# Two f blocks in one PSUM bank pair, transposes in other banks, and output products moved forward

## The chip, the cores and the metric

The kernel runs on one NeuronCore of a Trainium2 chip. The metric is the device time of one execution in microseconds (us), taken as the median of several runs. The engines have their own queues of instructions and meet only at semaphores: TensorE (PE) does the matmuls and its weight loads (PEld), VectorE (DVE), ScalarE (ACT) and GpSimd (POOL) the rest, and SyncE (SP) issues all large transfers, among them transposing ones. PE writes to PSUM, which has eight banks of 512 float32 columns here called 0 to 7; DVE and ACT read it.

## The reference

It is one transformer layer on 2048 tokens of width 448, with 16 heads of 28, in bf16. The first half is a linear attention whose features are two softmaxes, and the second a gated MLP of 1792 hidden columns:

```python
pq, pk = einsum(q, w_phi), einsum(k, w_phi)          # per head, 28 x 28
phi_q = concat([softmax(pq), softmax(-pq)]); phi_k = ...   # same for k
kv = einsum("bhsf,bhsd->bhfd", phi_k, v); z = einsum("bhsf->bhf", phi_k)
o = einsum("bhqf,bhfd->bhqd", phi_q, kv) / (einsum("bhqf,bhf->bhq", phi_q, z) + 1e-6)
h = x + o @ wo                                       # all of it on layernorm(x)
n = layernorm(h)
h2 = h + (sigmoid(n @ w_gate) * (n @ w_up)) @ w_down
```

## The kernel before, in words

The tokens are 16 tiles of 128, in four chunks of four tiles. Everything up to the sum kv (all keys and values) comes first, up to about 44 us. From there a tile passes through these named steps, whose names are those of the order lists:

- `pqa`/`pqb` c_i (function `pq`): the query features of chunk c, two groups of heads each, 512 columns, into banks 0 and 1 or 4 and 5. ACT takes two exponentials (`eq` with p or m) of the two banks together.
- `num` t: the products of a tile's query features with kv, into banks 6 and 7 (`num1` into 2 and 3). DVE makes `rsm`, `qq`, `b`, `c`, `rden` of it, and `o` t (DVE or POOL) writes the attention's output to o_pad. `oT` t transposes that, tiles 0 and 1 on PE, the others by a transfer that SP issues.
- `woa`/`wob` t: the output products of tiles t and t+1, banks 2 and 3. `h` t adds x (for tiles 0 and 1 the matmuls add it already); then come the second norm (`bs2`, `ag2` for tiles 0 and 1, `nm`, `sq`, `ve` for the others, `pow2` for the inverse root), `hn` t, and the transpose `hT` t, tiles 0 and 1 on PE, the others through SP.
- `ga`/`gb` t_f (function `gate_up`): gate and up products of one f block (128 of the 1792 hidden columns), 14 of them, for the tiles t on: tiles 0 and 1, and 2 and 3, in two phases of 256 tokens, the others in chunks of 512. Gate goes to bank 4 or 0, up to bank 5 or 1, by turns. `sig` t_f is a tanh on ACT into sg_sb (0.5 + 0.5 tanh(g/2) is the sigmoid), `hh` t_f on DVE makes (tanh + 1) times up, as bf16, in hhT.
- `dn`, `dp`, `dm` t_f (functions `down`, `down1`): the products with w_down, banks 2 and 3 for the early tiles, and `fin` t and `out` t, the second residual and the store.

Most products come as two halves. Matmuls use 64 rows of the array each, and two on opposite row halves run side by side (`both`, `pair`). The first half (`ga`, `pqa`, `woa`) has four such slots, with bank A on the low rows and bank B on the high rows; the second half (`gb`, ...) has three, with the rows swapped. A second half waits until the first half's matmuls into the same bank are complete (`crosses`, line 74).

The order on every engine is written out by hand in `ORDER` (lines 223 to 290). `PROGRAM` (line 292) gives the order in which steps are declared, and from that the waits come: a step waits for the last writer and the readers of each bank and tile that it writes, and the engines then go strictly by `ORDER`. So an instruction that waits holds back all that stand behind it on its engine.

In the phase of the first 256 tokens the order on PE is, with the gate products begun after both transposes:

```python
"pqa3_0 pqb3_0 wgu pqa3_1 num5 pqb3_1 hT1 hT0 num6 ga0_1 ga0_0 gb0_1 gb0_0 woa2 num7 ga0_2 ..."
```

The transposes `hT0`, `hT1` use banks 2 and 3, those of the output product just read. `wgu` does no work: it only makes PE wait for the gate and up weights.

Of the kernel before, what the change touches and what calls it, by code (L numbers as in the profile page):

```python
# [6 lines left out]
ALU = mybir.AluOpType  # L7
# [11 lines left out]
class Graph:  # L19
# [90 lines left out]
    def emit(self, nc):  # L110
# [85 lines left out]
P = 128  # L196
# [5 lines left out]
KT = 4  # L202
# [39 lines left out]
    ),  # L242
# [39 lines left out]
    ),  # L282
    "pool": (
# [5 lines left out]
    ),  # L289
}  # L290
PACE = {"ld_wg1": "kva14"}
PROGRAM = (
# [21 lines left out]

def pair(oa, ob, wa, wb, ra, rb):


    def f1(e):
        return both(e, [(oa, wa(LO, k), ra(LO, k), k == 0, False) for k in range(4)],
                    [(ob, wb(HI, k), rb(HI, k), k == 0, False) for k in range(4)])  # L320

    def f2(e):
        return both(e, [(ob, wb(LO, k), rb(LO, k), False, k == B_LO[-1]) for k in B_LO],
                    [(oa, wa(HI, k), ra(HI, k), False, k == A_HI[-1]) for k in A_HI])
    return f1, f2


def build(nc, A_x, A_wqkv, A_w_phi, A_wo, B_w_gate, B_w_up, B_w_down, out):
# [10 lines left out]
    with ExitStack() as es:  # L339
# [488 lines left out]
        def resid(t, b, ha=False):  # L828
# [27 lines left out]
            op("dve" if ha else ("dve", "pool"), "hn%d" % t, hnf, r=[("x", t), ("mv2", t) if ha else ("nm2", t), ("rst2", t)], w=[("hn", s)])  # L856
            if t < 2:
                pe_transpose("hT%d" % t, [hn_pad[:, s, kt * P:(kt + 1) * P] for kt in range(KT)], b, hnT[c][:, :, TS(t)],
                             ("hn", s), ("xnT", t))
            else:  # L860
                op("sp", "hT%d" % t, lambda e: e.dma_start_transpose(out=hnT[c][:, :, TS(t)], in_=hn_pad[:, s, :]),
                   r=[("hn", s)], w=[("xnT", t)], dma="tr", nring=64)

        def wout(t):
# [32 lines left out]
        for n, keys in (("wwo", wo_keys), ("wgu", wgu_keys)):  # L897
            op("pe", n, lambda e: None, r=keys, rows=64)
        sgn = [0]

        def gate_up(t0, n, ff):
            hb = hnT[t0 // 4]
            N = n * P
            ns = slice((t0 % 4) * P, (t0 % 4) * P + N)
            hk = [("xnT", t) for t in range(t0, t0 + n)]
            bg, bu = ((4, 5), (0, 1))[ff % 2]
            fs = slice(ff * P, (ff + 1) * P)
            nm = "%d_%d" % (t0, ff)
            f1, f2 = pair(bk(bg)[:, 0:N], bk(bu)[:, 0:N], lambda h, k: wg_sb[h, k, fs], lambda h, k: wu_sb[h, k, fs],
                          lambda h, k: hb[h, k, ns], lambda h, k: hb[h, k, ns])  # L910
            op("pe", "ga" + nm, f1, r=hk + wgu_keys, w=[B(bg), B(bu)], rows=64, half={bg: 0, bu: 1})
            op("pe", "gb" + nm, f2, r=hk + wgu_keys, w=[B(bg), B(bu)], rows=64, half={bg: 1, bu: 0})
            k = sgn[0] % NSG
            sgn[0] += 1
            op("act", "sig" + nm, lambda e: e.activation(sg_sb[:, k, 0:N], bk(bg)[:, 0:N], ACT.Tanh, scale=0.5), r=[B(bg)], w=[("sg", k)])  # L915
            op("dve", "hh" + nm, lambda e: e.scalar_tensor_tensor(out=hhT[(t0 // 4) % NHH][:, ff, ns], in0=sg_sb[:, k, 0:N], scalar=1.0,  # L916
                                                                  in1=bk(bu)[:, 0:N], op0=ALU.add, op1=ALU.mult),
               r=[B(bu), ("sg", k)], w=[("hh", (t0 // 4) % NHH, ff, t % 4) for t in range(t0, t0 + n)])

# [38 lines left out]
        for step in PROGRAM.split():  # L958
            k, _, v = step.partition(":")
            v = [int(i) for i in v.split(",") if i]  # L960
            if k == "num":
                num(*v)
            elif k == "wo":
                wout(v[0])
            elif k == "ot":
                otrans(v[0])
            elif k == "wo1":
                wout1(v[0])
            elif k == "qs":
                qsum(v[0])  # L970
            elif k == "pq":
                pq(*v)
            elif k == "kvz":
                kvmask()
            elif k == "gu":
                for ff in range(*(v[2:4] or (0, FT))):
                    gate_up(v[0], v[1], ff)
            elif k == "down":
                down(v[0], (v[1], v[1] + 1), mid)
            elif k == "down1":  # L980
                down1(v[0], v[1], late, *v[2:])
# [40 lines left out]
```

## Time and profile before

| | |
|---|---|
| median of 3 runs | 203.62 us (203.53 to 203.92) |
| profiled execution | 203.67 us, span 201.8 us |
| PE busy | 195.7 us, 97% of the span |
| DVE busy | 133.0 us, 66% |
| ACT busy | 91.3 us, 45% |
| POOL busy | 56.7 us, 28% |
| granted TensorE clock | 1.000 |
| gate products' start (`ga0_1`) | 59.24 us |
| first 512-column gate product (`ga4_1`) | 95.00 us |

The span is from the first to the last instruction. Times in the profile's rows count from the span's start. A row of the view in order of time has the start, the duration, the engine, the line, the operation, out<-in, and the count, and in brackets the idle time before it and what ended it. L311 is the helper through which all paired matmuls go, so the operands tell them apart: `xnT,Wq` are query products, `kvz,eq` nums, `wo_e` and `wo_o` output products, `xnT,wg_sb` and `xnT,wu_sb` gate and up, `wd_sb,hhT` down.

### The profile page before, as it was taken

How to read it: one execution, taken by the hardware profiler on the slowest of the kernel's cores; microseconds unless marked ns; L12 is line 12 of the kernel's file. 1: busy time of each engine (PE TensorE's matmuls, PEld its weight loads, DVE VectorE, ACT ScalarE, POOL GpSimd, SP SyncE). 2: the span in 40 equal slices, each digit the busy share in tenths (PEclk: the TensorE clock that was granted, in tenths of full speed). 3: DMA queues.
4: the chain of work that ended last, by engine and by line, in shares of the span. 5: the costliest groups of instructions: out<-in, count | busy, mean ns of one | idle time of the engine just before them, and what ended most of it. 6: DMA issues, size and time to landing. Idle time of an engine off the chain costs nothing.

```text
span 201.8 us, 5882 instructions
## 1 busy us (share of the span) xinstructions
PE 195.7 (97%) x2516; PEld 112.9 (56%) x2516; DVE 133.0 (66%) x320; ACT 91.3 (45%) x188; POOL 56.7 (28%) x97
## 2 busy tenths in 40 slices
PE   7999999999989999999999999999999999999995
PEld 3835656665558778676444444555555555554443
DVE  5999999978899677767758977436432422272224
ACT  2668898899772636222333442324422212222220
POOL 5879939433433614600041110001400000000000
PEclk9999999999999999999999999999999999999999
DMA  5965445839973320241005411030312000004003
GB/s 159 313 142 124 55 100 63 260 134 276 299 208 62 67 38 3 53 81 29 0 3 124 81 26 26 6 72 28 70 34 52 0 3 0 0 3 136 0 0 94
DMA packets 32491, 16.27 MB, mean 81 GB/s; under 512 B 24720, under 2 KB 31568, under 8 KB 32464
## 3 DMA queue, kind: packets, MB, share of 16 engines
q1 hardware_dynamic: 32336, 15.86, 32.4%
q8 instruction: 20, 0.33, 0.7%
q14 instruction: 7, 0.06, 0.1%
q10 hardware_dynamic: 128, 0.03, 0.1%
HBM read 8.34 MB, written 1.84 MB: 50 GB/s over the span
## 4 chain that ended last, share of the span: by engine, by line
PE 90%; ACT 2%; DVE 2%; DMA 2%; issue 1%; SPq 1%; POOL 1%
PE psum L311 83%; PE psum L943 5%; DMA wk_sb<-in_A_wqkv_dram 2%; ACT hhT L673 1%; ACT hhT L674 1%; PE psum L526 1%; PE psum L614 1%; SPq L415 1%; DVE st L831 1%; POOL rst L835 1%; PE psum L540 0%; DVE hn_pad L853 0%; DVE b_sb L803 0%; PE psum L601 0%; DVE c_sb L806 0%
## 5 line engine op out<-in xcount | busy, mean ns | idle before, releaser
L311 PE MATMUL psum<-xnT,wg_sb 64*128 64x512 bf16 (+1 forms) x490 | 93.1, 333 | 0.2
L311 PE MATMUL psum<-xnT,wu_sb 64*128 64x512 bf16 (+1 forms) x490 | 92.9, 333 | 0.0
L915 ACT ACTIVATE sg_sb<-psum 128x512 bf16<-128x512 f32 (+1 forms) x70 | 34.8, 511 | 91.3 <-PE psum L311 90.7
L916 DVE SCALAR_TENSOR_TENSOR hhT<-sg_sb,psum 128x512 bf16<-128x512 bf16 (+1 forms) x70 | 38.9, 576 | 54.5 <-ACT sg_sb L915 54.2
L311 PEld LDWEIGHTS psum<-xnT,wg_sb 64*128 64x128 bf16 x490 | 44.4, 94 | 22.5 <-DVE hhT L916 4.3
L311 PEld LDWEIGHTS psum<-xnT,wu_sb 64*128 64x128 bf16 x490 | 44.4, 94 | 13.0
L311 PE MATMUL psum<-wd_sb,hhT 64*128 64x448 bf16 x336 | 36.9, 349 | 0.0
L311 PEld LDWEIGHTS psum<-wd_sb,hhT 64*128 64x128 bf16 x336 | 17.6, 94 | 14.4 <-DVE x_sb L838 0.5
L311 PE MATMUL psum<-Wk,xnT 64*128 64x448 bf16 x112 | 22.2, 350 | 0.5 <-ACT hhT L674 0.2
L311 PE MATMUL psum<-wv_sb,xnT 64*128 64x448 bf16 x112 | 22.3, 351 | 0.1
L847 POOL TENSOR_SCALAR ve<-ssq 128x1 f32<-128x1 f32 x11 | 2.2, 201 | 55.0 <-ACT junk L844 54.8
L677 DVE TENSOR_REDUCE ss<-hhT 128x32 f32<-128x896 bf16 x16 | 16.9, 1066 | 0.6 <-ACT hhT L674 0.2
L723 ACT ACTIVATE eq<-psum 120x1024 bf16<-120x1024 f32 x16 | 15.7, 1024 | 1.0 <-PE psum L311 0.8
L687 POOL TENSOR_TENSOR phi<-hhT,rs 128x896 bf16<-128x896 bf16 x8 | 13.6, 1710 | 5.5 <-PE psum L311 5.1
L311 PE MATMUL psum<-xnT,Wq 64*120 64x512 bf16 x112 | 15.0, 384 | 0.1
L812 POOL TENSOR_TENSOR o_pad<-c_sb,rden 128x448 bf16<-128x448 bf16 x10 | 9.3, 935 | 14.9 <-DVE rden L808 14.8
L311 PE MATMUL psum<-wo_o,oT 64*128 64x448 bf16 x56 | 13.2, 349 | 0.0
L311 PE MATMUL psum<-wo_e,oT 64*128 64x448 bf16 x56 | 13.1, 349 | 0.0
L950 DVE SCALAR_TENSOR_TENSOR x_sb<-psum,x_sb 128x448 bf16<-128x448 f32 (+2 forms) x17 | 9.4, 592 | 2.7 <-PE psum L943 1.6
L943 PE MATMUL psum<-wd_sb,hhT 128*128 128x448 bf16 (+2 forms) x70 | 11.1, 316 | 0.0
L311 PEld LDWEIGHTS psum<-Wk,xnT 64*128 64x128 bf16 x112 | 7.8, 94 | 5.8 <-PE psum L311 1.0
L673 ACT ACTIVATE hhT<-psum 128x448 bf16<-128x448 f32 x16 | 8.8, 553 | 4.4 <-PE psum L311 4.2
(105 smaller groups left out, 235.4 us busy)
## 6 DMA issues: line engine op xcount, KB each, us to landing
out_dram<-x_sb SPq DMA_DIRECT2D x15, 112.0 KB, 1.8
x_sb<-in_A_x_dram SPq DMA_DIRECT2D x7, 224.0 KB, 3.9
wd_sb<-in_B_w_down_dram SPq DMA_DIRECT2D x7, 224.0 KB, 4.2
wg_sb<-in_B_w_gate_dram SPq DMA_DIRECT2D x3, 448.0 KB, 6.3
wu_sb<-in_B_w_up_dram SPq DMA_DIRECT2D x3, 448.0 KB, 6.7
wv_sb<-in_A_wqkv_dram SPq DMA_DIRECT2D x2, 224.0 KB, 4.7
wk_sb<-in_A_wqkv_dram SPq DMA_DIRECT2D x2, 196.0 KB, 3.8
wo_e<-in_A_wo_dram SPq DMA_DIRECT2D x1, 336.0 KB, 3.2
```

The lines of the kernel that those rows point to most:

```text
L311: p = e.matmul(o, lhsT=w, rhs=r, start=st, stop=sp, tile_position=(row, 0))
L415: return op(eng, name, lambda e: e.dma_start(dst, src), r=r, w=w, dma="in" if eng == "sp" else "ain", nring=48 if eng == "sp" else 8, kb=kb)
L673: e.activation(ek[:, s, :, 0, :], src, ACT.Exp)
L677: op("dve", "ss%d" % t, lambda e: e.tensor_reduce(ss[:, s, :].rearrange("p (b h) -> p b h", h=2), eks.rearrange("p b (d h) -> p b h d", h= ...
L687: return e.tensor_tensor(phi[:, sp, :, :, :].rearrange("p b a n -> p (b a) n")[:, :, 0:56].rearrange("p b (d h) -> p b d h", h=2), eks.rea ...
L723: op("act", "eq%d_%d%s" % (c, i, "pm"[sg]), lambda e, sg=sg: e.activation(eq[c][:, sg, 2 * i:2 * i + 2, :].rearrange("p g n -> p (g n)"), ...
L812: return e.tensor_tensor(o_pad[:, t % NO, off:off + D].rearrange("p (h d) -> p h d", h=H), c_sb[:, t % NS, :, 0:DH], rden[:, t % NS, :][:, ...
L847: op(("pool", "dve"), "ve%d" % t, lambda e: e.tensor_scalar(ve2[:, t:t + 1], ssq2[:, t:t + 1], 1.0 / D ** 3, EPS, op0=ALU.mult, op1=ALU.ad ...
L915: op("act", "sig" + nm, lambda e: e.activation(sg_sb[:, k, 0:N], bk(bg)[:, 0:N], ACT.Tanh, scale=0.5), r=[B(bg)], w=[("sg", k)])
L916: op("dve", "hh" + nm, lambda e: e.scalar_tensor_tensor(out=hhT[(t0 // 4) % NHH][:, ff, ns], in0=sg_sb[:, k, 0:N], scalar=1.0, in1=bk(bu)[ ...
L943: p = e.matmul(bk(b)[:, lo:hi], lhsT=hb[:, ff, TS(t)], rhs=wd_sb[:, ff, lo:hi], start=ff == 0, stop=ff == FT - 1)
L950: op("dve", "fin%d%s" % (t, nm), lambda e: e.scalar_tensor_tensor(out=h_sb[:, t, lo:hi], in0=bk(b)[:, lo:hi], scalar=0.5, in1=h_sb[:, t, l ...
```

## The change

In the two 256-token phases, an even and the next odd f block now share one bank pair: the even one uses columns 0 to 255 of the gate and the up bank, the odd one 256 to 511. The first matmul of the even block starts the banks, and the odd one's do not. The second halves `gb` of both blocks are declared after both first halves. One tanh and one `hh` of 512 columns then serve both, so `sig` and `hh` of odd f blocks are gone in these phases. The bank pairs go by turns of two blocks (4 and 5, then 0 and 1). The 512-token phases keep their form.

`hT0` and `hT1` move into a step of their own (`htrans`), declared after the query products of chunk 3's first groups, and use banks 0 and 1.

The order lists change from about 45 us to about 100 us: on PE `num1` stands before `pqb1_1`, `num4` between the halves of `pq3_0`, `num5` after `pqb3_1`, `woa2` before the first gate product, `num6` behind three of them, and `wgu` far back; the output products `woa`, `wob` and the down products come earlier among the gate products. DVE does the statistics, `hn` and transposes' copies of tile 1 before tile 0; ACT does `oT0e` one exponential earlier and `h1` before `h0`. `o7`, `hn2`, `hn3`, `nm2`, `nm3` and `ve3` go from POOL to DVE, and `o9`, `o10`, `ve5`, `ve7`, `nm5`, `nm9` and `hn7` from DVE to POOL. SP's order is the same.

```diff
-def pair(oa, ob, wa, wb, ra, rb):
+def pair(oa, ob, wa, wb, ra, rb, first=True, last=True):
...
-        return both(e, [(oa, wa(LO, k), ra(LO, k), k == 0, False) for k in range(4)],
+        return both(e, [(oa, wa(LO, k), ra(LO, k), first and k == 0, False) for k in range(4)],
...
-            if t < 2:
-                pe_transpose("hT%d" % t, [hn_pad[:, s, kt * P:(kt + 1) * P] for kt in range(KT)], b, hnT[c][:, :, TS(t)],
-                             ("hn", s), ("xnT", t))
-            else:
+            if t >= 2:
...
+        def htrans(t):
+            s = t % NH
+            pe_transpose("hT%d" % t, [hn_pad[:, s, kt * P:(kt + 1) * P] for kt in range(KT)], t, hnT[0][:, :, TS(t)], ("hn", s), ("xnT", t))
...
+            two = n == 2
-            bg, bu = ((4, 5), (0, 1))[ff % 2]
+            bg, bu = ((4, 5), (0, 1))[(ff // 2 if two else ff) % 2]
...
+            cs = slice(N * (ff % 2), N * (ff % 2) + N) if two else slice(0, N)
...
-            op("pe", "gb" + nm, f2, r=hk + wgu_keys, w=[B(bg), B(bu)], rows=64, half={bg: 1, bu: 0})
+            if two and ff % 2 == 0:
+                gate_up_b.append((nm, f2))
+                return
+            todo = gate_up_b + [(nm, f2)]
+            gate_up_b.clear()
+            for nb, fb in todo:
+                op("pe", "gb" + nb, fb, r=hk + wgu_keys, w=[B(bg), B(bu)], rows=64, half={bg: 1, bu: 0})
...
+            nm, W = todo[0][0], N * len(todo)
+            dst = hhT[(t0 // 4) % NHH][:, ff + 1 - len(todo):ff + 1, ns]
+            op("act", "sig" + nm, lambda e: e.activation(sg_sb[:, k, 0:W], bk(bg)[:, 0:W], ACT.Tanh, scale=0.5), r=[B(bg)], w=[("sg", k)])
...
 # order on PE from about 53 us (act, dve and pool likewise):
-pqa3_0 pqb3_0 wgu pqa3_1 num5 pqb3_1 hT1 hT0 num6 ga0_1 ga0_0 gb0_1 gb0_0 woa2 num7 ga0_2 ga0_3 gb0_2 gb0_3
-wob2 num8 ga0_4 ga0_5 gb0_4 gb0_5 woa4 ga0_6 ga0_7 gb0_6 gb0_7 wob4 ga0_8 ga0_9 gb0_8 gb0_9 woa6 ...
+pqa3_0 num4 pqb3_0 pqa3_1 pqb3_1 num5 hT1 hT0 woa2 ga0_2 ga0_0 ga0_1 num6 gb0_0 ga0_3 gb0_1 gb0_2 gb0_3 wob2 num7
+ga0_4 ga0_5 ga0_6 ga0_7 gb0_4 gb0_6 gb0_7 gb0_5 woa4 num8 wob4 ga0_8 ga0_9 ga0_10 gb0_8 gb0_9 woa6 ga0_11 wob6 ...
 # order on DVE:
-bs2_0 rsm4 bs2_1 qq4 ag2_0 ag2_1 b4 c4 hn0 hn1 rsm5 qq5 b5 hT1e c5 hT0e rden4 rsm6 rden5 qq6 b6 c6 hh0_1 hh0_0 rden6 ...
+bs2_1 bs2_0 rsm4 ag2_1 qq4 ag2_0 b4 hn1 c4 hn0 rden4 rsm5 hT1e qq5 hT0e b5 c5 rsm6 rden5 qq6 b6 c6 hh0_0 hh0_2 rsm7 rden6 qq7
+h2 b7 h3 c7 rden7 o7 hh0_4 ve3 hh0_6 h4 ...
```

More of the change, by code (lines that the diff above doesn't have):

```diff
@@ L312, in both @@
     return p
-def pair(oa, ob, wa, wb, ra, rb):
+def pair(oa, ob, wa, wb, ra, rb, first=True, last=True):
     def f1(e):
-        return both(e, [(oa, wa(LO, k), ra(LO, k), k == 0, False) for k in range(4)],
-                    [(ob, wb(HI, k), rb(HI, k), k == 0, False) for k in range(4)])
+        return both(e, [(oa, wa(LO, k), ra(LO, k), first and k == 0, False) for k in range(4)],
+                    [(ob, wb(HI, k), rb(HI, k), first and k == 0, False) for k in range(4)])
     def f2(e):
-        return both(e, [(ob, wb(LO, k), rb(LO, k), False, k == B_LO[-1]) for k in B_LO],
-                    [(oa, wa(HI, k), ra(HI, k), False, k == A_HI[-1]) for k in A_HI])
+        return both(e, [(ob, wb(LO, k), rb(LO, k), False, last and k == B_LO[-1]) for k in B_LO],
+                    [(oa, wa(HI, k), ra(HI, k), False, last and k == A_HI[-1]) for k in A_HI])
     return f1, f2
@@ L899, in build @@
         sgn = [0]
+        gate_up_b = []
         def gate_up(t0, n, ff):
@@ L905, in gate_up @@
             hk = [("xnT", t) for t in range(t0, t0 + n)]
-            bg, bu = ((4, 5), (0, 1))[ff % 2]
+            two = n == 2
+            bg, bu = ((4, 5), (0, 1))[(ff // 2 if two else ff) % 2]
             fs = slice(ff * P, (ff + 1) * P)
             nm = "%d_%d" % (t0, ff)
-            f1, f2 = pair(bk(bg)[:, 0:N], bk(bu)[:, 0:N], lambda h, k: wg_sb[h, k, fs], lambda h, k: wu_sb[h, k, fs],
-                          lambda h, k: hb[h, k, ns], lambda h, k: hb[h, k, ns])
+            cs = slice(N * (ff % 2), N * (ff % 2) + N) if two else slice(0, N)
@@ L911, in gate_up @@
+            f1, f2 = pair(bk(bg)[:, cs], bk(bu)[:, cs], lambda h, k: wg_sb[h, k, fs], lambda h, k: wu_sb[h, k, fs],
+                          lambda h, k: hb[h, k, ns], lambda h, k: hb[h, k, ns], not two or ff % 2 == 0, not two or ff % 2 == 1)
             op("pe", "ga" + nm, f1, r=hk + wgu_keys, w=[B(bg), B(bu)], rows=64, half={bg: 0, bu: 1})
-            op("pe", "gb" + nm, f2, r=hk + wgu_keys, w=[B(bg), B(bu)], rows=64, half={bg: 1, bu: 0})
+            if two and ff % 2 == 0:
+                gate_up_b.append((nm, f2))
+                return
@@ L913, in gate_up @@
+            todo = gate_up_b + [(nm, f2)]
+            gate_up_b.clear()
+            for nb, fb in todo:
+                op("pe", "gb" + nb, fb, r=hk + wgu_keys, w=[B(bg), B(bu)], rows=64, half={bg: 1, bu: 0})
             k = sgn[0] % NSG
             sgn[0] += 1
[L915 to L918, printed above, removed]
+            nm, W = todo[0][0], N * len(todo)
@@ new lines, in gate_up @@
+            dst = hhT[(t0 // 4) % NHH][:, ff + 1 - len(todo):ff + 1, ns]
+            op("act", "sig" + nm, lambda e: e.activation(sg_sb[:, k, 0:W], bk(bg)[:, 0:W], ACT.Tanh, scale=0.5), r=[B(bg)], w=[("sg", k)])
+            op("dve", "hh" + nm, lambda e: e.scalar_tensor_tensor(
+                out=dst, in0=sg_sb[:, k, 0:W].rearrange("p (f n) -> p f n", n=N), scalar=1.0,
+                in1=bk(bu)[:, 0:W].rearrange("p (f n) -> p f n", n=N), op0=ALU.add, op1=ALU.mult), r=[B(bu), ("sg", k)],
+               w=[("hh", (t0 // 4) % NHH, ff + 1 - len(todo) + i, t % 4) for i in range(len(todo)) for t in range(t0, t0 + n)])
@@ L964, in build @@
                 wout(v[0])
+            elif k == "ht":
+                htrans(v[0])
             elif k == "ot":
```

56 rows, old and new, of tables (ORDER, PROGRAM) are left out of this document.

## The prediction

> **What bounds the kernel now.** I read the page first, then the busy time by stretch, then the chain of waits around the stage that the change touches, and then the instructions there in order of time. The profiled execution took 203.67 us with a span of 201.8 us, so 1.9 us lie around the span; the median of the runs is 203.62 us, 0.05 us less. Against it 0.2% is 0.41 us, about what a measurement of this kernel can tell from no change.
>
> ```profile
> span 201.8 us, 5882 instructions
> PE 195.7 (97%) x2516; PEld 112.9 (56%) x2516; DVE 133.0 (66%) x320; ACT 91.3 (45%) x188; POOL 56.7 (28%) x97
> PE psum L311 83%; PE psum L943 5%; DMA wk_sb<-in_A_wqkv_dram 2%; ACT hhT L673 1%; ACT hhT L674 1%; PE psum L526 1%; PE psum L614 1%; SPq L415 1%; DVE st L831 1%; POOL rst L835 1%; PE psum L540 0%; DVE hn_pad L853 0%; DVE b_sb L803 0%; PE psum L601 0%; DVE c_sb L806 0%
> wu_sb<-in_B_w_up_dram SPq DMA_DIRECT2D x3, 448.0 KB, 6.7
> ```
> ```profile
> 45.60:53.30 7.70, 7.63 (x126) 4.37 (x128) 6.61 (x18) 7.01 (x8) 2.92 (x4) 1.00 0.99 311
> 53.30:59.24 5.94, 4.91 (x86) 2.79 (x83) 5.65 (x17) 4.96 (x7) 1.86 (x3) 1.00 0.91 193
> 59.24:95.00 35.76, 35.72 (x606) 27.09 (x608) 27.29 (x85) 14.02 (x41) 12.82 (x22) 1.00 0.27 58
> ```
>
> The columns of the second fence are the stretch, its length, and the busy time of PE, PEld, DVE, ACT and POOL. PE sets the end. The change removes no matmul, so it can only remove time in which PE waits. A busy PE hides short waits, because one matmul's time overlaps the next, so I count slots, the distance from start to start:
>
> ```profile
> 64.22 0.27 PE L311 MATMUL psum<-xnT,wg_sb 64*128 64x256 bf16 x1
> ...
> 64.98 0.27 PE L311 MATMUL psum<-xnT,wg_sb 64*128 64x256 bf16 x1
> ...
> 68.09 0.35 PE L311 MATMUL psum<-wo_o,oT 64*128 64x448 bf16 x1
> ...
> 68.47 0.35 PE L311 MATMUL psum<-wo_o,oT 64*128 64x448 bf16 x1
> ...
> 68.87 0.28 PE L311 MATMUL psum<-xnT,wg_sb 64*128 64x256 bf16 x1
> ```
> ```profile
> 52.10 0.35 PE L311 MATMUL psum<-wo_o,oT 64*128 64x448 bf16 x1
> 52.52 0.36 PE L311 MATMUL psum<-x_sb,ident 64*128 64x448 bf16 x2
> ```
> ```profile
> 56.24 0.40 PE L311 MATMUL psum<-kvz,eq 56*128 56x60 bf16 x16
> 56.48 0.83 PE L311 MATMUL psum<-xnT,Wq 64*120 64x512 bf16 x6
> 57.25 0.62 PE L540 MATMUL psum<-ident,hn_pad 128*128 128x128 bf16 x8
> 58.82 0.40 PE L311 MATMUL psum<-kvz,eq 56*128 56x60 bf16 x16 [0.94 <-DVE c_sb L806]
> 59.24 0.27 PE L311 MATMUL psum<-xnT,wg_sb 64*128 64x256 bf16 x1
> ```
>
> Two matmuls on opposite row halves share a slot. Seven slots of 256 columns last 64.98 - 64.22 = 0.76, or 0.109 each; two of 448 columns last 0.38, 0.19 each; a num product takes 56.48 - 56.24 = 0.24; three query slots of 512 columns last 0.65, 0.216 each; eight transposes 0.47. The last output slot at 68.47 should end at 68.66, and PE goes on at 68.87: 0.21 lost. At 52.10 the first half of an output product ends at 52.29, and its second half, into the same banks from the other row half, begins at 52.52: 0.23 lost, wherever two such halves stand side by side.
>
> From 53.30 to 59.24 PE has three nums (0.71), fourteen query slots (3.02) and eight transposes (0.47): 4.20 in 5.94, so 1.74 are lost. From 59.24 to 95.00 it has 28 f blocks of seven slots (21.3), 67 slots of 448 columns (12.7) and five nums (1.2): 35.2 in 35.76, so 0.55 are lost.
>
> ```profile
> 53.49 0.63 DVE st L831
> ...
> 55.02 1.09 POOL rst L835 x2
> ...
> 56.11 0.73 DVE hn_pad L853 x2
> ...
> 57.24 0.64 DVE b_sb L803
> 57.88 0.33 DVE xnT L533
> 58.22 0.56 DVE c_sb L806
> ```
>
> In the chain of waits the 1.74 us are a run of DVE and POOL steps: norm statistics, rstd, hn, transposes, then the product b, a copy, c, and only then num6 and the gate product.
>
> **The change part by part.** Durations for the replay, x being the count, then busy us and mean ns:
>
> ```profile
> L723 ACT ACTIVATE eq<-psum 120x1024 bf16<-120x1024 f32 x12 | 11.6, 1021 | 1.0 <-PE psum L311 0.8
> L916 DVE SCALAR_TENSOR_TENSOR hhT<-sg_sb,psum 128x512 bf16<-128x512 bf16 x16 | 10.8, 678 | 6.9 <-ACT sg_sb L915 6.7
> L916 DVE SCALAR_TENSOR_TENSOR hhT<-sg_sb,psum 128x256 bf16<-128x256 bf16 x28 | 10.7, 416 | 7.7 <-ACT sg_sb L915 7.7
> L803 DVE TENSOR_TENSOR b_sb<-psum,qq 128x464 bf16<-128x464 f32 x16 | 10.2, 637 | 0.7 <-PE psum L311 0.4
> L915 ACT ACTIVATE sg_sb<-psum 128x256 bf16<-128x256 f32 x28 | 9.8, 383 | 20.9 <-PE psum L311 20.9
> L915 ACT ACTIVATE sg_sb<-psum 128x512 bf16<-128x512 f32 x16 | 9.6, 597 | 22.2 <-PE psum L311 22.1
> L812 DVE TENSOR_TENSOR o_pad<-c_sb,rden 128x448 bf16<-128x448 bf16 x6 | 4.0, 665 | 0.1
> L533 DVE COPY xnT<-psum 128x512 bf16<-128x512 bf16 x2 | 0.8, 416 | 0.0
> ```
> ```profile
> 54.16 1.18 ACT L832 CAST x_sb<-psum 128x448 bf16<-128x448 f32 x2 [0.67 <-DVE st L831]
> 55.53 3.77 ACT L723 ACTIVATE eq<-psum 120x1024 bf16<-120x1024 f32 x4 [0.20 <-PE psum L311]
> ```
>
> *45.6 to 53.3.* num1 moves ahead of six query matmuls, so the exponentials behind these begin 0.24 later, and pqa2_1 waits 0.24 more for its banks. oT1 and num3 waited behind that already, for o1 and for c2, which come no earlier and no later; so the output product still begins at 51.3. The copy oT0e moved ahead of one exponential leaves ACT idle for about 0.6 until its transposes are done, and the last exponential of chunk 2 ends at about 53.8 instead of 53.5; pqa3_1 needs it only at 55.1. Cost 0; if both covers were gone, 0.24.
>
> *53.3 to the first gate product.* Replayed: pqa3_0 from 53.30 to 54.19; num4 stands between the halves and hides 0.23, to 54.42; pqb3_0 to 55.09. pqa3_1 to 55.96; its halves are now side by side, so 0.23 are lost, and pqb3_1 ends at 56.86: the two cancel. num5 to 57.10. DVE swaps the statistics and does hn1 after b4, hn0 after c4 (57.0); POOL's two rstd stand in the swapped order. The copies h1, h0 on ACT end at 55.2, the exponentials of pqa3_0 start at 55.3 behind pqb3_0 and free banks 0 and 1 at 57.26 (each 1.02, the second 0.92 after the first). The transposes hT1, hT0 now use these two banks, so they are the new wait: 57.36 to 57.83, 0.2 to 0.26 late. woa2 needs neither the copies nor num6 and fills 57.90 to 58.66 (four slots of 0.19), while DVE does hT1e, qq5, hT0e by about 58.7. ga0_2 starts at 58.75; ga0_0 needs the last exponential, 59.1, and comes at 59.2. c5 ends at 59.8, num6 comes at 60.1: no wait. Before, PE stood at 59.24 with num6 done and woa2 not. The lead is 59.24 - 58.75 + 0.76 - 0.24 = 1.0 us. What is late next is the exponential that frees bank 1.
>
> *Two f blocks in one bank pair.* Slots stay the same; the odd block's first matmuls go without the start flag, as three in seven did, at the same spacing: 0. Fourteen pairs of tanh (0.71 for two back to back, the row below) become fourteen of 0.60, and two hh of 0.42 each become one of 0.68. The price is that the bank pair comes free later: tanh starts some 0.21 after the last slot (below: a block whose slot at 65.32 ends at 65.43, its tanh at 65.63), then 0.60 and 0.68, 1.5 us in all, for both blocks together.
>
> ```profile
> 65.32 0.27 PE L311 MATMUL psum<-xnT,wg_sb 64*128 64x256 bf16 x1
> ```
> ```profile
> 65.63 0.71 ACT L915 ACTIVATE sg_sb<-psum 128x256 bf16<-128x256 f32 x2 [1.62 <-PE psum L311]
> ```
>
> What PE does from a pair's last slot to the next use of its banks, by the new order and the slots above: 1.46, 1.67, 1.56 us for the first three returns, then 2.8, 2.1, 2.8, 2.3, then 2.1, 1.8, 2.1, 2.5, 1.8 and 2.1 in the second phase and into the 512-token one. Only the first three are tight. hh0_0 stands right behind c6 (62.3) and ends at 62.95: ga0_4 waits 0.14. sig0_4 stands behind sq3, hh0_4 behind o7, ending at 67.7: ga0_8 waits 0.12. The third fits. About 0.1 elsewhere, where an output product meets DVE's h at 69.7 and 73.0 within 0.1. So of the 0.55 lost before, 0.35 remain: 0.2 gained. If every DVE step were ready, 0.5 gained; the bad end is a rival below.
>
> The Trainium skill, PSUM — Partial Sum Buffer, in its section on bank collisions, says to guard PSUM by bank and quadrant, not by address. That speaks against the change: the first block's half cannot be read while the second's is written. The trace of before has no bank with two blocks; by rows the sum is 0.2 gained with release in 1.5 us, and were a half free to be read early, the first waits would go and it would be about 0.5.
>
> *Queues.* SP's order stays. POOL gives o7, hn2, hn3 to DVE and takes o9, o10, nm5 and others; rden4 comes 2 us earlier, rden6 after hh0_2. oT7 is the tightest:
>
> ```profile
> L825 SPq DMA_TRANSPOSE oT<-o_pad x14: 1188/1199/1399, 52.2 to 131.1; - x14
> DMA to landing us min/median/max: 2.4/2.5/4.3
> ```
>
> o7 on DVE (0.67) ends at 66.9, oT7 lands 2.5 later at 69.4, woa6 needs it at 69.7: 0. At the median that holds; at 4.3 it costs 1.5. The hT2 and hT3 transposes land by 74.3 and ga2_2 comes at 75.3. wgu, the wait for the gate weights, moves behind their first use, so the gate product does the waiting; the last of them lands 6.7 after an issue at
>
> ```profile
> 46.29 0.43 SPq L415 DMA_DIRECT2D wu_sb<-in_B_w_up_dram x1
> ```
>
> that is at 53.0, before either place: 0. In the 512-token phases dp2_0 passes one gate half; no bank is short there, and I carry the lead through to the end.
>
> **Sum.** 0 + 1.0 + 0.2 = 1.2 us: 203.67 - 1.2 = 202.5 for the profiled run, 202.4 beside the median.
>
> **The rivals.**
> 1. *The in-order queues turn the shared banks into waits* (slower). If one b or c (0.64) stands ahead of each hh, release takes 2.14, and the returns above are short by 0.68, 0.47, 0.58, then 0, 0.04, 0, 0, 0.04, 0.34, 0.04, 0, 0.34, 0.04: 2.6 us. Against the 1.0 + 0.55 that would go otherwise, that is 1.05 slower: 204.7. It decides from about 0.45 us of delay at every return. For it: DVE is busy 27.29 of 35.76 us. Against: fourteen fewer instructions of each kind, and only the first two returns meet such a queue in the replay.
> 2. *The boundary gain goes to ACT* (same). If the exponentials come one place later (1.02, say because h1 and h0 wait longer for statistics), the transposes and ga0_0 move by as much, and of 1.2 some 0.2 is left: 203.4. For it: ACT is busy 4.96 of 5.94 us there. Against: those two copies need only DVE's first two steps.
> 3. *No new waits at all*: 1.74 + 0.55, less the 0.23 of the side-by-side halves, 2.06 gained: 201.6.
>
> **How the numbers follow.** Forecast 0.66, rival 1 0.14, rival 2 0.12 (most of it within 0.2%), rival 3 0.05, and 0.03 for a late oT7, 202.4 + 1.5 = 203.9, no change. So faster 0.72, same 0.14, slower 0.14. The range goes from rival 3's neighbourhood, 201.7, up to 203.3, where rival 2 begins; the forecast's own is 201.9 to 202.9.
>
> **What would show it.** Right: the gate product starts near 58.7 with woa2 before it; the idle 0.94 at num6 is gone; PE waits for hhT at the first two returns are 0.1 to 0.2 each; fourteen tanh and hh of 512 columns more, 28 of 256 fewer; the first 512-column gate product starts near 93.5 instead of 95.00 (the lead of 1.2, and dn2_8, 0.57, now behind it, num12, 0.24, ahead); later stages merely shift. Wrong: PE waits for hhT of 0.4 or more at several returns, transposes starting after 58, or the lead lost again behind 95.

## The result and the profile after

The changed kernel takes 202.33 us, median of 4 runs (202.17 to 202.70), against 203.77 (203.53 to 203.94) for the kernel before on the same chip: ratio 0.9933, with 95% confidence between 0.9914 and 0.9952, or 1.4 us faster (1.0 to 1.8). A second set of runs on another chip gave 202.50 (202.16 to 202.83), ratio 0.9934 [0.9916, 0.9952]. The profiled execution took 202.70 us.

The page of the changed kernel, parts 1, 4 and 5 (in part 5: x count, then busy us and mean ns, then idle time before and what ended it):

```profile
span 200.8 us, 5854 instructions
PE 195.5 (97%) x2516; PEld 114.4 (57%) x2516; DVE 132.0 (66%) x308; ACT 89.4 (45%) x174; POOL 56.2 (28%) x95
PE psum L309 84%; PE psum L954 5%; DMA wk_sb<-in_A_wqkv_dram 2%; ACT hhT L671 1%; ACT eq L721 1%; ACT hhT L672 1%; PE psum L524 1%; PE psum L538 1%; PE psum L612 1%; SPq L413 1%; PE psum L599 0%; ACT xnT L531 0%; ACT v L531 0%; DVE x_sb L961 0%
L925 ACT ACTIVATE sg_sb<-psum 128x512 bf16<-128x512 f32 x56 | 33.2, 596 | 90.1 <-PE psum L309 89.5
L926 DVE SCALAR_TENSOR_TENSOR hhT<-sg_sb,psum 128x512 bf16<-128x512 bf16 x56 | 37.7, 684 | 52.1 <-ACT sg_sb L925 51.7
```

PE has the same 2516 matmuls and the same busy time within 0.2 us. ACT and DVE have 14 and 12 instructions fewer (DVE takes nine steps from POOL, `nm6`, `nm7` and `ve4` besides the six named above, and gives it seven), and tanh and `hh` exist only in the 512-column form. Of the small steps in the old chain (`st`, `rst`, `hn_pad`, `b_sb`, `c_sb`) none stands in this line any more; the exponential `eq` L721 has come in.

The busy time by stretch, in the columns of the prediction's second fence:

```profile
45.86:53.61 7.75, 7.44 (x126) 4.38 (x127) 6.55 (x18) 6.73 (x8) 3.01 (x4) 1.00 1.03 322
53.61:59.01 5.40, 5.32 (x79) 3.05 (x75) 4.83 (x16) 4.84 (x7) 2.73 (x4) 1.00 1.06 207
59.01:93.70 34.69, 34.69 (x627) 28.21 (x626) 27.20 (x74) 12.54 (x28) 10.31 (x17) 1.00 0.34 58
```

Everything before the changed stage came 0.26 us later in this execution than in that of before (`num0` at 45.86 against 45.60; over the runs of this study it lies between 45.35 and 46.11). So from here on I measure D, the distance from `num0` to the first 512-column gate product, and correct it for the two steps that changed sides. Before: 95.00 - 45.60 = 49.40, less `dn2_8` (0.57), which now comes later, plus `num12` (0.24), which now comes sooner: D = 49.07. After: 93.70 - 45.86 = 47.84. That is 1.23 us gained; the prediction had 1.2.

In order of time on PE (start, duration, operation, out<-in, count):

```profile
56.48 0.86 PE L309 MATMUL psum<-xnT,Wq 64*120 64x512 bf16 x6
57.18 0.39 PE L309 MATMUL psum<-kvz,eq 56*128 56x60 bf16 x16
57.59 0.62 PE L538 MATMUL psum<-ident,hn_pad 128*128 128x128 bf16 x8
58.14 0.36 PE L309 MATMUL psum<-wo_e,oT 64*128 64x448 bf16 x1
...
58.72 0.35 PE L309 MATMUL psum<-wo_e,oT 64*128 64x448 bf16 x1
59.01 0.27 PE L309 MATMUL psum<-xnT,wg_sb 64*128 64x256 bf16 x1
...
62.88 0.39 PE L309 MATMUL psum<-kvz,eq 56*128 56x60 bf16 x16
63.24 0.28 PE L309 MATMUL psum<-xnT,wg_sb 64*128 64x256 bf16 x1
...
66.20 0.27 PE L309 MATMUL psum<-xnT,wg_sb 64*128 64x256 bf16 x1
66.44 0.35 PE L309 MATMUL psum<-wo_e,oT 64*128 64x448 bf16 x1
```

The transposes start at 57.59, the four slots of `woa2` at 58.14, and the gate product at 59.01, which is the predicted 58.75 plus the 0.26 of this execution. Before, PE stood still for 0.94 us in front of `num6`; now that time holds `woa2`. Two short losses can be read off: `num7` takes 0.24 from 62.88, so `ga0_4` could start at 63.12 and starts 0.12 later, and the slot at 66.20 ends at 66.31, while `woa4` starts at 66.44, 0.13 later.

The transposes start when ACT has freed banks 0 and 1. ACT in order of time:

```profile
54.48 1.06 ACT L830 CAST x_sb<-psum 128x448 bf16<-128x448 f32 x2 [0.50 <-DVE st L829]
55.60 3.77 ACT L721 ACTIVATE eq<-psum 120x1024 bf16<-120x1024 f32 x4
```

By the first to start and its length with the second, banks 0 and 1 are read by 57.53; `hT1` follows at 57.59, 0.18 behind the end of `num5` (57.18 + 0.23).

### The profile page after: what moved, and what is told of

It reads as the page before. It is cut to its first block, busy times and chain, and to the rows that moved or that the text cites. A ratio compares the mean times of both kernels' runs of the same rounds, so it can differ in the third digit from the quotient of the medians.

```text
span 200.8 us, 5854 instructions
## 1 busy us (share of the span) xinstructions
PE 195.5 (97%) x2516; PEld 114.4 (57%) x2516; DVE 132.0 (66%) x308; ACT 89.4 (45%) x174; POOL 56.2 (28%) x95
## 4 chain that ended last, share of the span: by engine, by line
PE 92%; ACT 3%; DMA 2%; issue 1%; SPq 1%; DVE 0%
PE psum L309 84%; PE psum L954 5%; DMA wk_sb<-in_A_wqkv_dram 2%; ACT hhT L671 1%; ACT eq L721 1%; ACT hhT L672 1%; PE psum L524 1%; PE psum L538 1%; PE psum L612 1%; SPq L413 1%; PE psum L599 0%; ACT xnT L531 0%; ACT v L531 0%; DVE x_sb L961 0%
## 5 line engine op out<-in xcount | busy, mean ns | idle before, releaser
L925 ACT ACTIVATE sg_sb<-psum 128x512 bf16<-128x512 f32 x56 | 33.2, 596 | 90.1 <-PE psum L309 89.5
L926 DVE SCALAR_TENSOR_TENSOR hhT<-sg_sb,psum 128x512 bf16<-128x512 bf16 x56 | 37.7, 684 | 52.1 <-ACT sg_sb L925 51.7
L810 POOL TENSOR_TENSOR o_pad<-c_sb,rden 128x448 bf16<-128x448 bf16 x11 | 10.2, 935 | 28.5 <-DVE rden L806 28.4
L721 ACT ACTIVATE eq<-psum 120x1024 bf16<-120x1024 f32 x16 | 15.6, 1030 | 0.6 <-PE psum L309 0.4
```

What stands on the lines that cost most here:

```text
L721: op("act", "eq%d_%d%s" % (c, i, "pm"[sg]), lambda e, sg=sg: e.activation(eq[c][:, sg, 2 * i:2 * i + 2, :].rearrange("p g n -> p (g n)"), ...
L810: return e.tensor_tensor(o_pad[:, t % NO, off:off + D].rearrange("p (h d) -> p h d", h=H), c_sb[:, t % NS, :, 0:DH], rden[:, t % NS, :][:, ...
L925: op("act", "sig" + nm, lambda e: e.activation(sg_sb[:, k, 0:W], bk(bg)[:, 0:W], ACT.Tanh, scale=0.5), r=[B(bg)], w=[("sg", k)])
L926: op("dve", "hh" + nm, lambda e: e.scalar_tensor_tensor(out=dst, in0=sg_sb[:, k, 0:W].rearrange("p (f n) -> p f n", n=N), scalar=1.0, in1= ...
```

## The experiments

Eleven other kernels were run, each against the kernel before on its own chip. In the fences the helper for paired matmuls is L308 to L310, depending on the kernel. The diffs show the order lists' tokens.

**1. Pairing alone.** Two f blocks per bank pair and the changed order behind the first gate products, with the boundary (everything from 45 to 59 us) as before.

```diff
 # from the changed kernel; act, dve, pool likewise
-... hT1 hT0 woa2 ga0_2 ga0_0 ga0_1 num6 gb0_0 ...
+... hT1 hT0 num6 ga0_2 ga0_0 ga0_1 woa2 gb0_0 ...   # all ahead of it as before, hT in banks 2 and 3
```

> The shared bank pairs with all that follows them, but the stage up to the first gate product as before: hT0 and hT1 in banks 2 and 3, num6 before the gate products, woa2 behind three of them. By the replay in the prediction the pairing alone gains about 0.2 us: 203.3 to 203.6, with num6 idle about 0.9 as before. If the gain came from the saved tanh and hh instructions, this kernel would keep most of it: 202.6 or less. If pairing alone costs time and the order at the boundary hides that, it is slower than before: 204.0 or more.

203.24 us against 203.54, ratio 0.9988 [0.9972, 1.0003]: 0.24 us faster by the ratio, where 0.2 had been predicted for pairing, though the interval just reaches no change. Its profiled execution took 203.66, longer than its median, for a reason of its own. PE in order of time:

```profile
55.64 0.64 PE L308 MATMUL psum<-xnT,Wq 64*120 64x512 bf16 x4 [0.23 <-DMA wu_sb<-in_B_w_up_dram]
```

Here the up weights landed at 55.40, and `wgu`, in its old place ahead of `pqa3_1`, held PE for them: by the starts, `pqa3_1` came 0.39 us late, and the first gate product 0.30 (13.95 behind `num0` instead of 13.64). D is 49.15; less these 0.30 it is 48.85, 0.22 below the 49.07 of before. So the old place of `wgu` is not free on every execution, which led to experiments 8 to 11.

**2 and 3. The boundary gain taken apart.** Experiment 2 puts the transposes back into banks 2 and 3, those of `woa2`. Experiment 3 keeps the new banks and puts `woa2` behind `num6`.

```diff
 # 2: in htrans
-kt in range(KT)], t, hnT[0]
+kt in range(KT)], 2 + t, hnT[0]
 # 3: order on PE
-hT0 woa2 ga0_2 ga0_0 ga0_1 num6 gb0_0
+hT0 ga0_2 ga0_0 ga0_1 num6 woa2 gb0_0
```

> The changed kernel with one edit: hT0 and hT1 go to banks 2 and 3 again, in the same place of the order. If the other banks are what lets the output product woa2 fill the wait, woa2 now waits for the copy hT0e (58.8 us in the changed kernel's trace), starts there instead of 58.14, and the first gate product comes 0.5 to 0.65 us later: 202.8 to 203.0, some 0.1 less if a later wait absorbs a part. If the banks do not matter, because the exponentials held the transposes back (hT1 waited until 57.59 for them) and now do not, the loss is 0 to 0.1.

> The changed kernel with woa2 behind num6 instead of ahead of the first gate product; the transposes keep banks 0 and 1. If the gain is that woa2 (0.76 us) fills the wait for the two copies, PE idles 0.85 us before the first gate product, which still starts at 59.0, and the kernel loses 0.76 less 0.14 to 0.27 that later waits (for oT5, for hh0_0) absorb: 202.8 to 203.0. If something else can fill or the chain behind is bound elsewhere, it loses under 0.2.

Experiment 2: 202.90 us, ratio 0.9968 [0.9957, 0.9979], D 48.50. Experiment 3: 202.94, ratio 0.9964 [0.9950, 0.9979], D 48.58. Each gives back somewhat more than half of the gain of 1.23, 0.66 and 0.74 us by D. PE in order of time, of experiment 2 and of experiment 3:

```profile
57.07 0.62 PE L538 MATMUL psum<-ident,hn_pad 128*128 128x128 bf16 x8
58.49 0.35 PE L309 MATMUL psum<-wo_e,oT 64*128 64x448 bf16 x1 [0.80 <-DVE xnT L531]
59.24 0.27 PE L309 MATMUL psum<-xnT,wg_sb 64*128 64x256 bf16 x1
```
```profile
57.73 0.62 PE L537 MATMUL psum<-ident,hn_pad 128*128 128x128 bf16 x8
59.15 0.27 PE L308 MATMUL psum<-xnT,wg_sb 64*128 64x256 bf16 x1 [0.80 <-DVE xnT L530]
```

Both have the same 0.80 us of idle PE, ended by the same thing, the copy of the transposed tile out of PSUM. In experiment 2 `woa2` itself waits for it, because it writes the banks that the copy reads (the transposes start earlier there, since these banks are free sooner); in experiment 3 nothing stands in the gap. So the two edits need each other: the free banks let `woa2` stand there, and `woa2` is what fills the wait.

**4. What is late next at the boundary.** One ACT copy of 0.62 us, which nobody reads, ahead of the first exponential of `pqa3_0`.

```diff
-h1 h0 eq3_0p eq3_0m
+h1 h0 slowa eq3_0p eq3_0m
```

> The changed kernel with one added ACT copy (about 0.5 us from start to start, nobody reads it) ahead of the exponentials of chunk 3's first groups. If ACT's exponentials are what is late next at the boundary, as the prediction says (rival 2), the transposes, the first gate product and the second come later by as much: 0.4 to 0.5 us slower, 202.7 to 202.9, with hT1 starting near 58.1. If DVE's chain or the output product's transfers hold the boundary, under 0.15.

202.95 us, ratio 0.9967 [0.9951, 0.9983], D 48.41: 0.57 us are lost, a little more than expected. The copy lasts 0.62 and makes the exponentials start 0.49 later (10.23 us behind `num0` instead of 9.74); the same 0.49 appear at `hT1` (12.22 instead of 11.73). PE in order of time:

```profile
57.59 0.62 PE L539 MATMUL psum<-ident,hn_pad 128*128 128x128 bf16 x8 [0.51 <-ACT eq L722]
```

PE now waits 0.51 for the exponential. "What is late next is the exponential that frees bank 1" holds, and with no slack, since the whole delay arrives: this is the mechanism of the second rival, and its price.

**5 and 6. The same delay at tight and at loose returns.** Three DVE instructions of 0.69 us, which compute something nobody reads, stand ahead of three `hh`: in experiment 5 those of the first three returns (1.46, 1.67 and 1.56 us by the prediction's list), in experiment 6 those of `hh0_8`, `hh0_10`, `hh0_12`, with 2.1 us and more.

```diff
 # 5
-hh0_0 ... hh0_2 ... hh0_4
+slow0 hh0_0 ... slow1 hh0_2 ... slow2 hh0_4
 # 6
-hh0_8 ... hh0_10 ... hh0_12
+slow0 hh0_8 ... slow1 hh0_10 ... slow2 hh0_12
```

> The changed kernel with three added DVE instructions of some 0.6 us each that nobody reads, one ahead of each of hh0_0, hh0_2 and hh0_4, the releases whose returns have 0 to 0.3 us of slack. If rival 1's price is right, each stands almost fully on PE's path: 1.5 to 1.9 us slower than the changed kernel, 203.8 to 204.2. If DVE's idle time (a quarter of that stretch) takes them up, under 0.4: 202.7 or less.

> The same three added DVE instructions, ahead of hh0_8, hh0_10 and hh0_12, whose returns have 0.5 to 1.3 us of slack in the prediction's list. If the slack of each return decides, they cost 0 to 0.3 us: 202.3 to 202.6. If DVE's total work decides, they cost as much as at the tight returns.

Experiment 5: 204.38 us (203.84 to 206.07) against 203.85, ratio 1.0034 [1.0010, 1.0059], D 49.58: the added work costs 1.74 us in the trace and about 2 by the ratios to before, more than the whole change had gained, and the median lies just above the expected range. Experiment 6: 202.66, ratio 0.9944 [0.9925, 0.9963], D 48.23: the same work costs 0.39 us in the trace, somewhat above the 0 to 0.3 expected, and about 0.2 by the ratios, which their intervals can't tell from nothing. Of its 0.39, 0.25 stand at `ga2_2`, which uses the banks that `hh0_10` frees, and 0.15 at `woa2`, which has nothing to do with the edit (it waited for `oT3`; see below). So 0.25 is the price of the edit. DVE of experiment 5 in order of time, and its waits of PE from 58 to 72 us (total, times, longest):

```profile
61.99 0.69 DVE L932 SCALAR_TENSOR_TENSOR scr<-zero 128x512 bf16<-128x512 bf16 x1
62.59 0.68 DVE L926 SCALAR_TENSOR_TENSOR hhT<-sg_sb,psum 128x512 bf16<-128x512 bf16 x1
```
```profile
PE psum L308 <- DVE ve L845: 0.8, 1, 0.8
PE psum L308 <- DVE hhT L926: 0.7, 2, 0.6
```

The first row is the added instruction, straight ahead of `hh0_0` on its engine. The view names two releasers, the banks' `hh` and another DVE step (a wait for several is put down to the one that came last by the profile); counted by slots, PE lost 0.72, 0.32 and 0.95 at the three returns. So sharing a bank pair does turn into waits where DVE is late by about half a microsecond, as the first rival had it. In the changed kernel the same returns cost 0.12, 0 and 0 us.

**7. The oT5 wait.** The loss of 0.13 at `woa4` was not in the prediction. `oT5`, the transposing transfer that `woa4` needs, was issued at 62.17 and landed at 66.35. Experiment 7 makes `rden5` one place earlier, so that the transfer is issued earlier.

```diff
-c5 rsm6 rden5 qq6
+c5 rden5 rsm6 qq6
```

> The changed kernel with one DVE instruction moved: rden5 ahead of rsm6, which waits 0.68 us for num6. The chain rden5, o5, oT5 then starts about 0.8 us earlier. If woa4's wait of 0.14 us at 66.3 was for oT5's landing (66.35), that wait goes: 0.1 us faster, 202.2, below what the timing can tell, so the trace decides: no gap before woa4. If the wait was for h3 or for the transfer queue, the gap stays.

202.47 us, ratio 0.9939 [0.9922, 0.9957], D 47.83: nothing gained. PE and DVE in order of time:

```profile
66.27 0.27 PE L308 MATMUL psum<-xnT,wg_sb 64*128 64x256 bf16 x1
66.38 0.35 PE L308 MATMUL psum<-wo_e,oT 64*128 64x448 bf16 x1
...
67.75 0.35 PE L308 MATMUL psum<-wo_o,oT 64*128 64x448 bf16 x1
68.06 0.28 PE L308 MATMUL psum<-xnT,wg_sb 64*128 64x256 bf16 x1
```
```profile
67.33 0.68 DVE L925 SCALAR_TENSOR_TENSOR hhT<-sg_sb,psum 128x512 bf16<-128x512 bf16 x1
```

`oT5` lands at 63.92 and `woa4` follows its neighbour in one slot of 0.11. But the slot at 67.75 ends at 67.94 and `ga0_8` starts at 68.06, behind `hh0_4`, which ends at 68.0: 0.12 lost. That is the wait that the prediction had at `ga0_8`. In the changed kernel the stop at `woa4` covers it: the late transfer and the late `hh0_4` (which ends at 67.94 there, `ga0_8` at 68.01) end one and the same loss of 0.13, so that taking one of the two away gains nothing.

**8 to 11. The place of wgu.** The change moves `wgu` behind the first use of the weights, at a predicted cost of 0. Experiment 8 is the kernel before with only that move, experiment 9 is experiment 1 with it; experiments 10 and 11 are the changed kernel with `wgu` between `num5` and `hT1`, and in its old place ahead of `pqa3_1`.

```diff
 # 8 and 9: order on PE
-pqb3_0 wgu pqa3_1
+pqb3_0 pqa3_1
-gb4_3
+wgu gb4_3
 # 10, from the changed kernel
-num5 hT1 ... ga4_2 wgu gb4_3
+num5 wgu hT1 ... ga4_2 gb4_3
 # 11, from the changed kernel
-pqb3_0 pqa3_1 ... ga4_2 wgu gb4_3
+pqb3_0 wgu pqa3_1 ... ga4_2 gb4_3
```

> The kernel before with one edit: wgu, which makes PE wait for the gate and up weights, moves from ahead of pqa3_1 to the place it has in the changed kernel, so that the first gate product does the waiting. The prediction put this at 0, since the weights land at 53 to 54 us. In the profiled run of the pairing alone they landed at 55.40, and PE stood 0.39 us ahead of pqa3_1. If that happens in many executions, this kernel is 0.1 to 0.3 us faster than before; if it is rare, it is the same within 0.1.

> The kernel with the pairing alone and the stage up to the first gate product as before, with the same edit to wgu. By the replay the pairing is worth 0.2 us, and wgu what the run beside this one shows: 0.2 to 0.4 us faster than before, 203.1 to 203.3. In the trace no gap of 0.4 ahead of pqa3_1, and from num0 to the first 512-column gate product 0.2 less than before.

Experiment 8: 203.77 us against 203.54, ratio 1.0007 [0.9992, 1.0021]. Experiment 9: 203.51, ratio 0.9997 [0.9983, 1.0011], D 49.06. Neither gains, where 0.2 to 0.4 had been expected of experiment 9, though PE can no longer wait for the weights at `pqa3_1`. PE of experiment 8 in order of time:

```profile
59.32 0.40 PE L310 MATMUL psum<-kvz,eq 56*128 56x60 bf16 x16 [0.94 <-DVE c_sb L805]
59.97 0.27 PE L310 MATMUL psum<-xnT,wg_sb 64*128 64x256 bf16 x1 [0.24 <-ACT eq L722]
```

From `num6` to the gate product it is 0.65 us, where the kernel before has 59.24 - 58.82 = 0.42. The weights had landed at 54.59, so it is not the transfers that PE waits for: the gate product has taken over the waits on the eight weight transfers (`wgu_keys`), and where PE has just stood still and has nothing queued these cost it 0.23 us. In experiment 9 the same 0.22 takes just what pairing gives. The row names ACT as what ended the idle time. The exponentials end at 59.81 here, but in the kernel before the gate product started at 59.24, ahead of their end at 59.30, so it does not need the last of them. That it is the waits themselves is inferred from the one edit that separates the two kernels, twice.

> The changed kernel with one edit: wgu stands between num5 and hT1, where PE waits for the exponentials anyway, instead of far behind. If the wait instructions for eight loads cost PE time when they stand at the first gate product (0.22 us more ahead of it in the two kernels with wgu moved and the old boundary), they are hidden here: the first gate product comes 0.06 us after the copy hT0e instead of 0.15, 0.1 us faster than the changed kernel beside it, which the times may just show. If the landing of the weights or the copy is what is late, nothing changes.

> The changed kernel with wgu ahead of pqa3_1, its place in the kernel before. Between num5 and hT1 the eight wait instructions moved their cost instead of hiding it (0.09 us later transposes for 0.09 us less ahead of the first gate product). Ahead of pqa3_1 PE has query products queued on both sides and the weights have landed a microsecond earlier, so the cost should vanish: 0.09 us less from num0 to the first 512-column gate product than the changed kernel's 47.84. If the weights land after 55.3 in this execution, the first half of the last query product waits for them.

> The changed kernel itself, on the same chip as the run beside it: 202.2 to 202.5.

These three went to two chips. Experiment 10: 202.34 us against 202.50 for the changed kernel beside it, ratios to before 0.9932 [0.9915, 0.9949] and 0.9934 [0.9916, 0.9952]; D 47.84 and 47.83. No difference. PE and DVE of experiment 10 in order of time:

```profile
56.77 0.39 PE L308 MATMUL psum<-kvz,eq 56*128 56x60 bf16 x16
57.28 0.61 PE L537 MATMUL psum<-ident,hn_pad 128*128 128x128 bf16 x8
...
58.40 0.35 PE L308 MATMUL psum<-wo_e,oT 64*128 64x448 bf16 x1
58.59 0.28 PE L308 MATMUL psum<-xnT,wg_sb 64*128 64x256 bf16 x1
```
```profile
58.12 0.42 DVE L530 COPY xnT<-psum 128x512 bf16<-128x512 bf16 x1
```

The gate product now follows the copy by 0.05 us (58.54 to 58.59) instead of 0.15 (58.86 to 59.01 in the changed kernel), and the last output slot at once (58.40 + 0.19) instead of 0.1 later (58.72 + 0.19). But the transposes start 0.51 behind `num5` instead of 0.41: the waits have only changed place. Experiment 11: 203.01 us (202.23 to 203.61), ratio 0.9966 [0.9952, 0.9981], where 0.09 had been expected as a gain. PE of experiment 11 in order of time:

```profile
57.25 0.62 PE L537 MATMUL psum<-ident,hn_pad 128*128 128x128 bf16 x8
58.62 0.35 PE L308 MATMUL psum<-wo_e,oT 64*128 64x448 bf16 x1 [0.74 <-DMA oT<-o_pad]
```

The transposes come 11.73 behind `num0`, 0.09 earlier than in experiment 10 and as in the changed kernel, but `woa2` waits 0.74 for `oT3`, which was issued at 54.00 and landed only at 58.48 (D 48.53). In the changed kernel itself `oT3` landed at 57.24 and 56.89 in its two profiled executions, against `woa2` at 58.14 and 58.24. Whether the old place of `wgu` costs time in the other executions of experiment 11, or late landings alone do, stays open: only one execution has a trace.

The boundary change without pairing was not tried; its order of all queues would have been a new one. No version ran faster than the changed kernel beyond the interval.

## Why the prediction was right

Measured 202.33, forecast 202.4; in the profiled execution the gain between `num0` and `ga4_1` is 1.23 against a sum of 1.2. (The whole profiled execution took 202.70 where 202.5 was forecast; 0.26 of that had gone before `num0`.) Step by step:

- **45.6 to 53.3, cost 0, at most 0.24.** The product after the output products (`pqa3_0`, before `num4`) started 7.75 us behind `num0` instead of 7.69, so 0.06. The copies hide nearly all, not all.
- **To the first gate product, 1.0.** From `num0` it was 13.64 with `num6` done and `woa2` not, and is 13.15 with `woa2` done and `num6` not: 0.49 + 0.76 - 0.24 = 1.01, the 0.06 above included. Experiments 2 and 3 show that it hangs on both edits, experiment 4 that the exponentials are next. The cancelling pair (0.23 hidden by `num4`, 0.23 lost at `pqa3_1`) is in the trace with that size: `pqa3_1` shows a gap of 0.22 between its halves. That the gate product itself starts just when forecast, at 59.01 for 58.75 + 0.26, is partly chance: the copy ahead of it ended at 58.86, 0.1 before the forecast's 58.7 + 0.26, and the waits of `wgu`, forecast at 0, took that 0.1.
- **Pairing, 0.2.** By the prediction's count of slots, 59.01 to 93.70 has 28 f blocks (21.3), 60 slots of 448 columns (11.4) and seven nums (1.7): 34.4 in 34.69, so 0.3 are lost where 0.35 had been expected, of the 0.55 before. The wait at `ga0_4` has 0.12 against 0.14. In place of the 0.12 at `ga0_8` there is 0.13 at `woa4`, which was not forecast; experiment 7 shows that the two are one loss with two ends, and that they end so close together is chance. Experiment 1 has 0.24 for pairing alone. Experiments 5 and 6 bear out the list of returns: the first three are tight, the others are not. From the end of a pair's last slot to the end of its `hh` the changed kernel takes 1.51 to 1.55 us at ten of the fourteen pairs, as forecast (1.5), but 2.35 at `hh0_10`, which stands behind other DVE steps; of that return of 2.8 only 0.5 was slack, and there experiment 6 lost its 0.25. (By the kernel before, six in seven of the matmuls into a bank go without the start flag, not three; an odd block's four slots, at `ga0_1`, still take 0.44.)
- **The release of a shared bank.** The Trainium skill, PSUM — Partial Sum Buffer, in its section on bank collisions, has PSUM guarded by bank and quadrant, not by address. The changed kernel keeps to that (a release after both blocks), and no run here reads one half while the other is written, so what an early read would do is not shown.
- **Queues, 0.** The direction held, the terms did not. For `oT7` it held: it landed at 69.79 for a predicted 69.4 + 0.26, and `woa6` started at 69.98. But it was not "the tightest". `oT5` landed at 66.35, 4.18 behind its issue, and `woa4` waited for it. And `woa2`, which starts 2.9 us earlier behind `num0` than before, stands 0.1 to 1.4 us behind the landing of `oT3` in the traces that have it ahead of the gate products (0.9 in the profiled execution; experiment 2, where it waits for the copy, left out), and in experiments 6 and 11 it waited. The step that failed is the landing time: the median of 2.5 is that of the whole run, while the four `oT` transfers between 52 and 64 us read in the changed kernel

```profile
DMA to landing us min/median/max: 2.9/4.2/4.4
```

  The first three of these run beside weight loads. `oT5` hardly does: the last load landed at 62.33, `oT5` was issued at 62.17, and in experiment 7, issued at 61.48, it took 2.44. The fourteen traces of this study agree in one thing: in the nine with a long `oT5` (3.9 to 4.3 us) a 16 KB packet of the queue that the page calls `instruction` runs for about 1 us just ahead of the last packets of `oT5` (64.36 to 65.32 in the changed kernel), and in the five with a short one (2.4 to 2.5) the packets of `oT5` are done before it. No run changes that alone, so the cause is not shown.

- **wgu, 0.** Mis-sized, by little: about 0.1 in the changed kernel (between the last output slot and the gate product), and 0.22 with the old boundary. What it saves is the wait that experiment 1 met, 0.39 when the weights land late. The landing was mis-sized as well: the forecast's 53.0 takes the page's median of 6.7, while in the trace of before the last up weights landed 7.7 behind their issue, at 54.00. That was still ahead of `pqa3_1` at 55.33; the 55.40 of experiment 1 was not.
- **Carried to the end.** The last stop of the 512-token phases, at `ga8_1`, is 0.27 in both traces, and the lead arrives at the end.

The first rival did not come about: PE's waits for `hh` are 0.12 at one return and not 0.4 at several. Experiment 5 shows that it was a real alternative with a price near the predicted one: three instructions of 0.69 cost 1.74 in all, where that rival's count gives 0.68, 0.47 and 0.58, or 1.73, for a delay of 0.64. The single returns (0.72, 0.32 and 0.95) differ more. The second rival did not come about because the copies `h1` and `h0` kept their place in time; experiment 4 shows that one ACT step more would have cost 0.57.

## What to carry to other kernels

A wait on the critical engine is worth filling before it is worth shortening: look for work in its queue that needs none of the late results, and see whether only a shared buffer keeps it from standing there; here the moved buffer without the moved work kept 0.49 of the 1.23 us, and the moved work without the moved buffer 0.57, the 0.2 of pairing included. When two blocks share a buffer to save instructions, list for every reuse the time from the last write to the next, set it against the release time, and order the releasing engine for the few entries that are short. When work moves forward, check its transfers against landing times in that stretch, not against the median of the run.

## What was not expected of the hardware

- Transposing transfers of the same size took 2.4 us from issue to landing at `oT7`, in every trace, and 2.5 to 5.8 at `oT2` and `oT3`, in the stretch with the weight loads; the landing of `oT3` varied between 56.4 and 58.5 us over the executions of these kernels, which is more than the margin that `woa2` has.
- Waits on eight transfers that had long landed cost PE 0.22 to 0.23 us where it came from a standstill (experiments 8 and 9), and 0.1 in the changed kernel; both are read from kernels that differ in the place of `wgu` alone.
- Experiment 5, with delays at the tight returns, had the widest spread: 203.84 to 206.07 over ten runs, where the changed kernel has 202.16 to 202.83 over ten. Why is not shown.
